# A decode attention kernel: the output matrix wo in four even loads in place of strips over chosen rows

## The chip, the cores and the metric

The kernel runs on one core of one Trainium2 chip. The metric is the device time of one execution in microseconds (us), from the chip's own clock; the median of several runs is given, and the runs of one kernel agree closely. The profile of one execution gives, beside that, its span: the time from its first to its last instruction.

## What is computed

One token passes through an attention block over a cache of 4096 keys and values with 32 heads (A), and through a small MLP with a squared ReLU (B); a sigmoid gate mixes the two.

```
x: 1 x 512; k_cache, v_cache: 32 heads x 4096 x 128; wq: 512 x 4096; wo: 4096 x 512
g = sigmoid(sum(x * gate_w))
q = x @ wq                              # 32 heads of 128
p = softmax(q . k_cache * 128 ** -0.5)  # one row of 4096 for each head
o = p @ v_cache                         # 32 x 128
a = o.reshape(1, 4096) @ wo
h = relu(x @ w1 + b1); b = (h * h) @ w2 + b2       # w1: 512 x 1376
out = g * a + (1 - g) * b
```

All tensors are bf16. The two caches are 33.6 MB each; `wq` and `wo` are 4 MB each, `w1` and `w2` 1.4 MB each.

## The kernel before

The 32 heads are worked in eight quads of four (`NQ`, `R`). A quad's keys are one load of 128 partitions with 32 KB each, and so are its values; the tile `KV` has four slots for them, and `ORDER` gives the order in which SP's queue issues the sixteen loads. A load waits until the load four places earlier has been used up (`done`): for keys until VectorE (DVE) and TensorE (PE) have read them, for values until the product with the probabilities (`pv`) is done.

Half of each quad's scores are made by DVE (`ttr`: multiply and sum of a 128 x 128 block with the query), half by PE: `transposes` into PSUM, a copy by ScalarE (ACT, `evac`), and `scores`. Then follow the maximum (`smax`, `max_rows`, `gmax`, `max_cols`), the exponentials on ACT (`exps`), the denominators (`den`) and `pv` on PE, and `recip` and `norm` on DVE, which leave the four heads' results, times the gate, as four columns of `onorm` (128 x 32, one column a head). Each engine runs its list in order, so where a call stands in the loop over quads and over the eight groups `g` of blocks decides what waits behind it. `PV_BEHIND` says behind which quad each `pv` comes; the last three quads' values are used after the loop.

Before `wo` can be applied, `onorm` has to be laid out as the rows of `wo` lie in SBUF. `wo` has 4096 rows of 1 KB. In this kernel

- rows of heads 0 to 22 (`HX` = 23) go to the tile `W`, whose space the query weights `wq` have left by then. They form 92 strips of 32 KB: a strip is one partition of `W`, with sixteen rows of the lower and sixteen rows of the upper half. Not every partition has a strip. `RUNS` lists 14 loads of strips that GpSimd (POOL) issues, `FIRST` five that SP issues, each with a class `e`, a count, a remainder and a multiple; `place` turns these into partitions. The classes count from 0 to 15 and stand for groups of eight partitions: `32 + 4e + r` and `4e + r` for `e` below 8, `64 + 4e + r` for the outer runs above. POOL issues small loads in between (`dm`, L374), as many rows of 32 bytes as `turns` says, and waits for them at its end;
- rows of head 23 go to `wox`, and those of heads 24 to 31 to `wob_sb` (8 KB on each of 128 partitions), both in a slot of `KV` that the fifth quad's values have left; SP issues them after the last values.

Because the strips' places are irregular, DVE builds at its start a table of which strip lies on which partition (`ramp`, `qv`, `hrow`, `crow`), PE spreads it with three products (L477 to L479), DVE copies it (`sel`), and two comparisons (`mask`, L751) in quad 2 turn it into the selection table `selA`. POOL builds a second, regular one, `selB`, with a memset and an affine select. The result is then brought into place in three parts: `turn_low`, `spread_low` and `out_a(True)` for the lower half in quads 5 and 6; `turn_a`, `spread_a` and `out_a(False)` for the upper half after `pv(5)`; `regroup`, `out_b` and `out_x` after the last `pv`. A turn is a transpose of columns of `onorm` and a copy; a spread is 8 or 16 products with the selection table and a copy; `out_*` are products of 128 x 128 blocks of `wo` with one column, summed in `acc`.

`w1` follows the first values on SP's queue, `w2` comes in five parts (`W2_PARTS`): the first ahead of the last values, the others at the end of the queue. `mlp_out` and `mlp_rows` add the MLP's part to `acc` and `acc4`; a last product turns the sum, DVE copies it to `fin4`, and SP stores it.

The issue order on SP around the change:

```
for n in range(len(ORDER)):
    if n == len(ORDER) - 1:
        load_w2(0)
    load_kv(n)
    ...
    if 4 <= n < 4 + len(FIRST):
        load_first(n - 4)
done("V", NQ - 4)
eng.dma_start(wob_sb, wob_v).then_inc(s_wo, 16)
load_w2(1)
eng.dma_start(wox, A_wo[HX * 128:NA * 128, :]).then_inc(s_wx, 16)
```

Of the kernel before, what the change touches and what calls it, by code (L numbers as in the profile page):

```python
# [5 lines left out]
def bass_gated_mix__gqa_block_cached__dense_activation_squared_relu__decode_kernel(  # L6
# [15 lines left out]
    fp32 = mybir.dt.float32  # L22
# [5 lines left out]
    NH = 32  # L28
# [22 lines left out]
    NA = 24  # L51
    TB = 8

# [6 lines left out]
    W_SLOT = V_SLOT[NQ - 4]  # L60
# [4 lines left out]
    INNER, OUTER, SEAM, WRAP = range(4)  # L65
    RUNS = [(INNER, 4, 12, 0, 2), (INNER, 4, 12, 1, 2),
            (OUTER, 4, 3, 0, 1), (SEAM, 7, 2, 0, 1), (OUTER, 9, 7, 0, 1),
            (SEAM, 7, 2, 1, 1), (WRAP, 15, 2, 1, 1), (OUTER, 1, 2, 1, 1), (OUTER, 3, 2, 1, 1),
            (SEAM, 7, 2, 2, 1), (WRAP, 15, 2, 2, 1), (OUTER, 1, 2, 2, 1),
            (SEAM, 7, 2, 3, 1), (WRAP, 15, 2, 3, 1)]  # L70
    FIRST = [(INNER, 0, 3, 0, 1), (INNER, 0, 3, 1, 1), (INNER, 0, 3, 2, 1), (INNER, 0, 3, 3, 1),
             (OUTER, 0, 2, 0, 1)]
    HX = NA - 1

    NS2 = 4 * HX

    def place(kind, e, k, r, m):
        if kind == INNER:
            return 32 + 4 * e + r, 4 // m, k * m
        if kind == OUTER:  # L80
            return (4 * e if e < 8 else 64 + 4 * e) + r, 4, k
        if kind == SEAM:
            return 28 + r, 68, k
        return r, 124, k

    def turns():
        at, out = 0, []
        for _, e, k, _, _ in RUNS:
            d = (e - at) % 16
            out.append((False, d) if d != 1 else (True, e))  # L90
            at = (e + k) % 16
        return out

    def strips():
        q = 0
        for run in RUNS + FIRST:
            yield (*place(*run), q)
            q += place(*run)[2]

    STRIPS = list(strips())  # L100

# [8 lines left out]
    woa_v = A_wo[0:HX * 128, :].rearrange("(a p t) n -> p a (t n)", a=2, t=16)  # L111
    wob_v = A_wo[NA * 128:NH * 128, :].rearrange("(p t) n -> p t n", t=TB)
# [4 lines left out]
    with ctx:  # L117
# [12 lines left out]
        W2 = W[:, :].rearrange("p (a x) -> p a x", a=2)  # L130
        wo_sb = W[:, :].rearrange("p (t n) -> p t n", t=32)
        wob_sb = KV[:, W_SLOT, 0:TB * DM].rearrange("p (t n) -> p t n", t=TB)
        wox = KV[:, W_SLOT, TB * DM:(TB + 1) * DM]
# [3 lines left out]
        selB = w1_sb[0:NH - NA, 0:2, 0:1024].rearrange("h a (c p) -> h a c p", c=8)  # L137
        selA = w1_sb[0:NA, 2:4, 0:1024].rearrange("h a (c p) -> h a c p", c=8)
# [8 lines left out]
        oA = sb("oA", [NA, 128], bf16)  # L147
        oL = sb("oL", [NA // 2, 128], bf16)
        oB = sb("oB", [NH - NA, 128], bf16)
        o2A = sb("o2A", [128, 32], bf16)  # L150
        o2B = sb("o2B", [128, TB], bf16)
# [3 lines left out]
        dm = xb[:, :, :].rearrange("p t (n a c) -> p (t n) a c", a=2, c=16)  # L155
# [5 lines left out]
        ramp = S[0:1, 0, :]  # L161
        qv = S[0:1, 1, :]
        hrow = S[0:1, 2, 0:NA]
        crow = S[0:1, 2, 32:48]
        sel = sb("sel", [NA, 144], fp32)
# [26 lines left out]
        SEL = pO[0:NA, 256:400]  # L192
# [3 lines left out]
        O2A = pS[0][:, 0:16]  # L196
        OL = pQ[0:NA // 2, 0:64].bitcast(bf16)
        O2L = pQ[:, 64:80]
        O2B = pS[1][:, 0:TB]
# [10 lines left out]
        s_wr = sem("s_wr")  # L210
        s_wx = sem("s_wx")
# [4 lines left out]
        s_wo = sem("s_wo")  # L216
        s_wp = [sem(f"s_wp{n}") for n in range(len(RUNS))]
        s_dm = [sem(f"s_dm{n}") for n in range(len(RUNS))]
# [38 lines left out]
        s_at = sem("s_at")  # L257
        s_ra = sem("s_ra")
        s_qv = sem("s_qv")
        s_sp = sem("s_sp")  # L260
        s_sc = sem("s_sc")
        s_sa = sem("s_sa")
        s_lt = sem("s_lt")
        s_lc = sem("s_lc")
        s_ac = sem("s_ac")
        s_oT = sem("s_oT")
        s_oc = sem("s_oc")
        s_o2 = sem("s_o2")
# [25 lines left out]
        def _(eng):  # L294
# [23 lines left out]
            def load_first(n):  # L318
                if n == 0:
                    eng.wait_ge(s_qps, NQ)  # L320
                p, st, k, q = STRIPS[len(RUNS) + n]
                eng.dma_start(W2[p:p + st * (k - 1) + 1:st, :, :], woa_v[q:q + k, :, :],
                              max_dma_last_dim=16384).then_inc(s_wr, 16)
# [8 lines left out]
# [4 lines that stand above are left out]
                if n == 2:  # L336
                    eng.wait_ge(s_z, 1)
                    eng.wait_ge(s_b2, 1)
                    eng.dma_start(w1_sb[:, :, :], w1_v[:, :, :]).then_inc(s_w1, 16)
                if 4 <= n < 4 + len(FIRST):  # L340
                    load_first(n - 4)
            done("V", NQ - 4)
            eng.dma_start(wob_sb, wob_v).then_inc(s_wo, 16)
            load_w2(1)
            eng.dma_start(wox, A_wo[HX * 128:NA * 128, :]).then_inc(s_wx, 16)
# [8 lines left out]
        def _(eng):  # L354
# [11 lines left out]
            eng.wait_ge(s_qps, NQ)  # L366
            q = 0
            sent = 0
            for n, ((back, d), run) in enumerate(zip(turns(), RUNS)):
                if back:  # L370
                    eng.inc_swdge_sem([], [], mode="reset_dge_cursor")
                if d:
                    src = B_w1[0:d, 0:32].rearrange("p (a c) -> p a c", a=2)
                    eng.dma_start(dm[0:d, sent, :, 0:8], src[:, :, 0:8]).then_inc(s_dm[sent], 16)  # L374
                    sent += 1
                p, st, k = place(*run)
                eng.dma_start(W2[p:p + st * (k - 1) + 1:st, :, :], woa_v[q:q + k, :, :],  # L377
                              max_dma_last_dim=16384).then_inc(s_wp[n], 16)
                q += k
            assert q == STRIPS[len(RUNS)][3] and STRIPS[-1][3] + STRIPS[-1][2] == NS2  # L380
            eng.wait_ge(s_h, 1)
            eng.memset(w1_sb[0:NH - NA, 0:2, 0:1024], 0.0).then_inc(s_sb, 1)
# [4 lines left out]
            for n in range(sent):  # L387
                eng.wait_ge(s_dm[n], 16)
# [6 lines left out]
        def _(eng):  # L395
# [44 lines left out]

            for c in range(QF):
                qb_copy(c)
# [4 lines left out]
            for q in range(NQ):  # L447
                for g in range(GQ):
# [7 lines left out]
                    if g == 5 and q >= 1:  # L456
                        exps(q - 1)
                s_copy(q)
                if q == NQ - 3:
                    eng.wait_ge(s_lt, 1)  # L460
                    eng.activation(oL[:, :], OL, ACT.Copy).then_inc(s_lc, 1)
                    eng.wait_ge(s_lt, 2)
                    eng.activation(o2A[:, 0:16], O2L, ACT.Copy).then_inc(s_lc, 1)
# [4 lines left out]
        def _(eng):  # L468
# [6 lines left out]
            eng.wait_ge(s_qv, len(STRIPS) + 4)  # L475
            eng.wait_ge(s_xf, 1)
            eng.matmul(SEL[:, 0:128], onesf[0:1, 0:NA], qv, start=True, stop=True)  # L477
            eng.matmul(SEL[:, 128:144], hrow, onesf[0:1, 0:16], start=True, stop=False)
            eng.matmul(SEL[:, 128:144], onesf[0:1, 0:NA], crow, start=False, stop=True).then_inc(s_sp, 1)  # L479
# [86 lines left out]
            def turn_low():  # L566
                eng.wait_ge(s_on, 3)
                eng.wait_ge(s_hs, 2)
                eng.transpose(OL, onorm[:, 0:NA // 2], ident[:, :]).then_inc(s_lt, 1)

            def spread_low():
                eng.wait_ge(s_lc, 1)
                eng.wait_ge(s_sb, 2)
                eng.wait_ge(s_sa, 2)
                for c in range(8):
                    mm = eng.matmul(O2L, selA[0:NA // 2, 0, c, :], oL[:, 16 * c:16 * c + 16],
                                    start=(c == 0), stop=(c == 7))
                mm.then_inc(s_lt, 1)

            def turn_a():  # L580
                eng.wait_ge(s_on, NA // R)
                eng.wait_ge(s_ev, GQ * NQ)
                eng.transpose(KP[2][0:NA, 0:128], onorm[:, 0:NA], ident[:, :]).then_inc(s_at, 1)

            def spread_a():
                eng.wait_ge(s_ac, 1)
                eng.wait_ge(s_cp, R * (NQ - 1))
                for c in range(8):
                    mm = eng.matmul(O2A, selA[:, 1, c, :], oA[:, 16 * c:16 * c + 16],
                                    start=(c == 0), stop=(c == 7))  # L590
                mm.then_inc(s_at, 1)

            def out_a(low):
                if low:
                    eng.wait_ge(s_lc, 2)
                    for q in s_wp:
                        eng.wait_ge(q, 16)
                    eng.wait_ge(s_wr, 16 * len(FIRST))
                else:
                    eng.wait_ge(s_ac, 2)  # L600
# [293 lines left out]
```

## Time and profile before

| what | us or share |
|---|---|
| median of 3 runs | 193.64 (193.63 to 193.68) |
| the profiled execution's own time | 193.59 |
| its span | 192.2 |
| DVE busy | 129.0 (67%) |
| PE busy | 124.2 (65%) |
| ACT busy | 99.3 (52%) |
| POOL busy | 19.9 (10%) |
| read from HBM | 78.32 MB, 407 GB/s over the span |

The profile's slices cut the span into forty equal parts; a digit is the busy share in tenths. The row DMA is the mean over the core's sixteen DMA engines, the row under it what they moved. In the windows the columns are the stretch, its length, busy time and count of PE, PE's weight loads, DVE, ACT and POOL, the clock granted to PE, the DMA share and GB/s. The chain of waits goes back from the last instruction, at each step to what released it. Queue q1 holds the loads that SP issues, q0 those of GpSimd, q10 four small ones of ACT; q8 and q14 bring the engines' instructions. Beside these views the trace keeps every DMA packet (start, duration, size, queue) and each step of each load's semaphore, sixteen for a load over 128 partitions.

### The profile page before, as it was taken

What the parts mean: (1) busy time and instruction counts of PE and PEld (TensorE: products, weight loads), DVE (VectorE), ACT (ScalarE), POOL (GpSimd) and SP (SyncE); (2) the same over time, 40 slices, a digit from 0 to 9 for tenths busy, and PEclk for the clock granted to TensorE, in tenths of its full rate; (3) what the DMA queues carried; (4) which work ended last, traced back from release to release, by engine and by line L of the source; (5) the groups of instructions that cost most, each with busy time, mean ns of one, the idle gap of its engine ahead of it and who ended that gap; (6) DMA issues with size and microseconds to landing.
All of it is one profiled execution on the core that took longest, in us unless ns stands there. A gap on an engine that the chain in (4) does not pass through costs nothing.

```text
span 192.2 us, 6534 instructions
## 1 busy us (share of the span) xinstructions
PE 124.2 (65%) x2439; PEld 111.4 (58%) x2441; DVE 129.0 (67%) x1120; ACT 99.3 (52%) x214; POOL 19.9 (10%) x37
## 2 busy tenths in 40 slices
PE   0047378793898826473992849279569667756746
PEld 0023256672888716463991849179569566656635
DVE  1340399999605999999989649999987992100010
ACT  3007289899403897258199119969816963100000
POOL 5000000029946100000000000000000000000000
PEclk9999879788555885555588557957955975555555
DMA  6999999999999999999999999999999999999990
GB/s 218 437 436 436 436 438 426 436 390 446 453 408 440 423 426 423 425 436 413 425 419 426 418 433 430 428 431 433 423 435 433 416 428 426 430 382 418 420 355 28
DMA packets 5118, 78.73 MB, mean 410 GB/s; under 512 B 1349, under 2 KB 1831, under 8 KB 2088
## 3 DMA queue, kind: packets, MB, share of 16 engines
q1 hardware_dynamic: 4050, 75.76, 92.9%
q0 software_dynamic: 1024, 2.56, 3.4%
q8 instruction: 19, 0.31, 0.7%
q14 instruction: 11, 0.09, 0.1%
q10 hardware_dynamic: 14, 0.01, 0.0%
HBM read 78.32 MB, written 0.00 MB: 407 GB/s over the span
## 4 chain that ended last, share of the span: by engine, by line
DMA 48%; DVE 23%; PE 12%; ACT 10%; issue 4%; SPq 1%; DVEq 0%; ACTq 0%
DMA KV<-in_A_k_cache_dram 34%; DVE KV L776 19%; DMA w2a<-in_B_w_dram 14%; ACT kT L419 6%; PE KP L505 6%; PE pO L549 2%; ACT E L437 2%; PE pQ L487 1%; DVE w_sb L751 1%; PE pS L517 1%; DVE S L776 1%; SPq L299 1%; PE pO L646 1%; ACT qb L408 0%; ACT S L425 0%
## 5 line engine op out<-in xcount | busy, mean ns | idle before, releaser
L776 DVE CUSTOM_DVE_ANT_0 KV<-KV,qb 128x128 bf16<-128x128 bf16 x512 | 112.0, 285 | 14.6 <-DMA KV<-in_A_k_cache_dram 14.6
L419 ACT ACTIVATE kT<-KP 128x1024 bf16<-128x1024 bf16 x64 | 62.0, 1025 | 39.5 <-PE KP L505 38.2
L505 PE MATMUL KP<-ident,KV 128*128 128x128 bf16 x512 | 51.0, 268 | 6.4 <-DMA KV<-in_A_k_cache_dram 6.4
L505 PEld LDWEIGHTS KP<-ident,KV 128*128 128x128 bf16 x512 | 42.5, 123 | 8.6 <-DMA KV<-in_A_k_cache_dram 4.1
L517 PE MATMUL pS<-qcol,kT 128*128 128x4 bf16 x512 | 23.5, 167 | 25.3 <-ACT kT L419 24.7
L776 DVE DVE_READ_ACCUMULATOR2_ANT S<- 128x1 f32 x512 | 39.5, 77 | 0.0
L517 PEld LDWEIGHTS pS<-qcol,kT 128*128 128x128 bf16 x512 | 20.7, 103 | 28.0 <-ACT kT L419 27.5
L549 PEld LDWEIGHTS pO<-E,KV 128*128 128x128 bf16 x1024 | 29.4, 105 | 6.6 <-DMA KV<-in_A_v_cache_dram 4.9
L549 PE MATMUL pO<-E,KV 128*128 128x4 bf16 x1024 | 29.1, 166 | 6.1 <-DMA KV<-in_A_v_cache_dram 4.6
L437 ACT ACTIVATE E<-S,nM 32x128 bf16<-32x128 f32 x32 | 18.5, 577 | 0.9
L408 ACT ACTIVATE qb<-pQ 32x128 bf16<-32x128 f32 x20 | 5.4, 268 | 12.6 <-PE pQ L487 12.2
L798 DVE RECIPROCAL rden<-pO 128x4 f32<-128x4 f32 x7 | 1.2, 173 | 14.4 <-PE pO L549 14.4
L374 POOL DMA_DIRECT2D xb<-in_B_w_dram x9 | 5.4, 604 | 38.5 <-PE pQ L487 38.5
L425 ACT ACTIVATE S<-pS 32x64 f32<-32x64 f32 x32 | 6.9, 215 | 4.3 <-PE pS L517 3.7
L437 ACT ACTIVATION_READ_ACCUMULATOR E<-S,nM 32x1 f32 x32 | 8.0, 251 | 0.0
L487 PE MATMUL pQ<-W,xb 128*128 128x512 bf16 x18 | 6.8, 515 | 1.7 <-ACT qcol L413 1.2
L377 POOL DMA_DIRECT2D W<-in_A_wo_dram x14 | 7.9, 565 | 0.0
L477 PE MATMUL pO<-S,onesf 1*24 1x128 f32 x2 | 0.6, 410 | 9.4 <-DVE S L742 9.4
L804 DVE SCALAR_TENSOR_TENSOR onorm<-pO,gcol,rden 128x4 bf16<-128x4 f32 x8 | 1.8, 222 | 6.2 <-PE pO L549 5.9
L525 PE MATMUL pM<-identf,mp 128*1 128x128 f32 x8 | 3.0, 372 | 4.2 <-DVE mp L784 4.2
L477 PEld LDWEIGHTS pO<-S,onesf 1*24 1x24 f32 x2 | 0.1, 119 | 9.5 <-DVE S L742 9.5
L529 PE MATMUL pM<-onesf,dg 1*128 1x1 f32 x16 | 3.4, 281 | 3.0 <-DVE dg L791 3.0
(108 smaller groups left out, 85.3 us busy)
## 6 DMA issues: line engine op xcount, KB each, us to landing
KV<-in_A_k_cache_dram SPq DMA_DIRECT2D x8, 4096.0 KB, 30.3
KV<-in_A_v_cache_dram SPq DMA_DIRECT2D x7, 4096.0 KB, 25.0
W<-in_A_wq_dram SPq DMA_DIRECT2D x1, 4096.0 KB, 12.2
KV<-in_A_v_cache_dram SPq DMA_DIRECT2D x4, 1024.0 KB, 21.1
W<-in_A_wo_dram POOLq DMA_DIRECT2D x2, 768.0 KB, 19.5
w_sb<-in_B_w_dram SPq DMA_DIRECT2D x1, 1376.0 KB, 12.0
w2a<-in_B_w_dram SPq DMA_DIRECT2D x2, 512.0 KB, 28.0
KV<-in_A_wo_dram SPq DMA_DIRECT2D x1, 1024.0 KB, 26.3
```

Source lines behind the costliest of these rows:

```text
L374: eng.dma_start(dm[0:d, sent, :, 0:8], src[:, :, 0:8]).then_inc(s_dm[sent], 16)
L377: eng.dma_start(W2[p:p + st * (k - 1) + 1:st, :, :], woa_v[q:q + k, :, :], max_dma_last_dim=16384).then_inc(s_wp[n], 16)
L408: eng.activation(qb[rows(r), c, :], QR[c][rows(r), r * 128:(r + 1) * 128], ACT.Copy)\
L419: eng.activation(kT[:, n % NT, :], KP[n % 3][:, :], ACT.Copy).then_inc(s_ev, 1)
L425: eng.activation(S[rows(r), q % NS, 0:YQ], S2[rows(r), :, r], ACT.Copy).then_inc(s_cp, 1)
L437: eng.activation(E[rows(r), q % NE, :, r], S[rows(r), q % NS, :], ACT.Exp, bias=nM[rows(r), q:q + 1], scale=SCALE, accum_out=RS[rows(r), h ...
L487: mm = eng.matmul(QR[c], xb[:, t, :], wq_sb[:, t, c * 512:(c + 1) * 512], start=(t == 0), stop=(t == 3))
L505: mm = eng.transpose(KP[n % 3][:, y * 128:(y + 1) * 128], key(q, b), ident[:, :])
L517: mm = eng.matmul(pS[q % 2][:, R * c:R * c + R], kT[:, n % NT, y * 128:(y + 1) * 128], qcol[:, R * q:R * q + R], start=True, stop=True)
L529: eng.matmul(MB[:, q:q + 1], dg[:, q % 2, :], onesf[0:1, 0:1], start=True, stop=True).then_inc(s_mb, 1)
L549: mm = eng.matmul(O[:, R * q:R * q + R], KV[:, V_SLOT[q], b * 128:(b + 1) * 128], E[:, q % NE, COLUMN[b], :], start=(b == 0), stop=(b == N ...
L776: ins = eng.tensor_tensor_reduce(key(q, b), key(q, b), qb[:, q, :], 1.0, 0.0, ALU.mult, ALU.add, S[:, q % NS, c:c + 1])
```

## The change

`wo` is cut into four groups of eight heads (`NG`, `GH`), and each group is one load of 1 MB over 128 partitions with 8 KB runs, all four into `W`. SP issues groups 0, 1 and 2 behind V1, K4 and V2 (`WO_AT`), group 3 behind the last values; head 23's own load is gone. POOL's 14 strip loads and 9 small ones go, and so do DVE's table, PE's three products for it and the comparisons. One selection table, `selB`, serves all groups. Groups 0 and 1 are turned, spread and multiplied in quads 5 and 7 (`GROUP_IN`), with ACT's copies; group 2 after `pv(5)` and group 3 after the last `pv`, with DVE's copies. Turn and spread write into the bank `pM`.

```diff
+    NG = 4
+    GH = NH // NG
+    GROUP_IN = {5: 0, 7: 1}
+    WO_AT = {5: 0, 6: 1, 7: 2}
...
-    woa_v = A_wo[0:HX * 128, :].rearrange("(a p t) n -> p a (t n)", a=2, t=16)
-    wob_v = A_wo[NA * 128:NH * 128, :].rearrange("(p t) n -> p t n", t=TB)
+    wo_v = A_wo.rearrange("(g p t) n -> g p t n", g=NG, t=TB)
...
+        wo_sb = W[:, :].rearrange("p (g t n) -> p g t n", g=NG, t=TB)
...
-            def load_first(n):
-                if n == 0:
-                    eng.wait_ge(s_qps, NQ)
-                p, st, k, q = STRIPS[len(RUNS) + n]
-                eng.dma_start(W2[p:p + st * (k - 1) + 1:st, :, :], woa_v[q:q + k, :, :],
-                              max_dma_last_dim=16384).then_inc(s_wr, 16)
+            def load_wo(g):
+                if g == 0:
+                    eng.wait_ge(s_qps, NQ)
+                eng.dma_start(wo_sb[:, g, :, :], wo_v[g, :, :, :]).then_inc(s_wo[g], 16)
...
-                if 4 <= n < 4 + len(FIRST):
-                    load_first(n - 4)
-            done("V", NQ - 4)
-            eng.dma_start(wob_sb, wob_v).then_inc(s_wo, 16)
+                if n in WO_AT:
+                    load_wo(WO_AT[n])
+            load_wo(NG - 1)
             load_w2(1)
-            eng.dma_start(wox, A_wo[HX * 128:NA * 128, :]).then_inc(s_wx, 16)
...
+            def turn(g, nm):
+                eng.wait_ge(s_on, 2 * g + 2)
+                eng.wait_ge(s_nm, nm)
+                eng.transpose(OT, onorm[:, GH * g:GH * g + GH], ident[:, :]).then_inc(s_ot, 1)
+
+            def spread(g):
+                eng.wait_ge(s_oc, 2 * g + 1)
+                if g == 0:
+                    eng.wait_ge(s_sb, 2)
                 for c in range(16):
+                    mm = eng.matmul(O2, selB[:, c // 8, c % 8, :], oT[:, g, TB * c:TB * c + TB],
                                     start=(c == 0), stop=(c == 15))
+                mm.then_inc(s_ot, 1)
+
+            def out_rows(g):
+                eng.wait_ge(s_oc, 2 * g + 2)
+                eng.wait_ge(s_wo[g], 16)
+                if g == 0:
+                    eng.wait_ge(s_hs, 2)
                 for t in range(TB):
                     for j in range(4):
+                        eng.matmul(acc[:, j:j + 1], wo_sb[:, g, t, j * 128:(j + 1) * 128], o2[:, g, t:t + 1],
+                                   start=(g == 0 and t == 0 and j == 0), stop=False, skip_group_check=True)
...
+                    if g == 6 and q in GROUP_IN:
+                        turn(GROUP_IN[q], q)
+                    if g == 7 and q in GROUP_IN:
+                        spread(GROUP_IN[q])
+                if q in GROUP_IN:
+                    out_rows(GROUP_IN[q])
...
-            turn_a()
-            spread_a()
-            out_a(False)
+            turn(NG - 2, NQ)
+            spread(NG - 2)
+            out_rows(NG - 2)
...
-            regroup()
-            out_b()
+            turn(NG - 1, NQ)
+            spread(NG - 1)
+            out_rows(NG - 1)
             mlp_out(1)
-            out_x()
...
+            def ot_copy(g):
+                eng.wait_ge(s_ot, 2 * g + 1)
+                eng.activation(oT[:, g, :], OT, ACT.Copy).then_inc(s_oc, 1)
...
+            def group(g):
+                eng.wait_ge(s_ot, 2 * g + 1)
+                eng.tensor_copy(oT[:, g, :], OT).then_inc(s_oc, 1)
+                eng.wait_ge(s_ot, 2 * g + 2)
+                eng.tensor_copy(o2[:, g, :], O2).then_inc(s_oc, 1)
```

On ACT, `ot_copy` and `o2_copy` (the same for `O2` into `o2`) stand behind the evacuations of groups 6 and 7 of quads 5 and 7.

## The prediction

> **What bounds the kernel now.** I read the page's slices first, then the windows by stage, the DMA queues, the chain that ended last, and at the end the single packets and landings in the trace.
>
> ```profile
> span 192.2 us, 6534 instructions
> ...
> DMA  6999999999999999999999999999999999999990
> GB/s 218 437 436 436 436 438 426 436 390 446 453 408 440 423 426 423 425 436 413 425 419 426 418 433 430 428 431 433 423 435 433 416 428 426 430 382 418 420 355 28
> ...
> q1 hardware_dynamic: 4050, 75.76, 92.9%
> q0 software_dynamic: 1024, 2.56, 3.4%
> q8 instruction: 19, 0.31, 0.7%
> q14 instruction: 11, 0.09, 0.1%
> ```
>
> ```profile
> 41.50:125.00 83.50, 54.59 (x1045) 51.96 (x1042) 69.91 (x602) 51.13 (x102) 17.21 (x25) 0.65 1.01 427
> 125.00:158.70 33.70, 25.47 (x554) 24.45 (x555) 31.75 (x290) 23.36 (x48) 0.00 (x0) 0.70 1.01 430
> 158.70:184.20 25.50, 16.65 (x506) 15.56 (x504) 2.46 (x12) 2.49 (x9) 0.00 (x0) 0.50 0.99 414
> 184.20:189.50 5.30, 4.06 (x108) 3.50 (x109) 0.76 (x4) 0.00 (x0) 0.00 (x0) 0.50 0.63 226
> ```
>
> The reader is to see that the DMA engines are busy from the first slice to the last but one (last columns of the windows: share 1.01, 1.01, 0.99). No compute engine is: DVE, the busiest, stands at 67%. The chain of waits names DVE and PE often, but behind each sits a K or V load that was waiting in a full queue. Its end is plain:
>
> ```profile
> 160.96 27.32 DMA w2a<-in_B_w_dram
> 188.27 0.05 issue
> 188.32 0.59 PE pQ L637 x16
> ```
>
> So bytes in flight set the end, and the bytes stay: `wo` is 4 MB before and after. What changes is **which DMA engine carries how much**, so I went down to single packets. A 32 KB row takes 1.214 us on one engine (median of 2048), a 16 KB piece 0.612, an 8 KB one 0.313, a 1 KB one 0.046, a semaphore write 0.009. A load of 128 rows puts eight rows on each of sixteen engines; I call these lanes and number them by the classes `e` in `place`. For every load the trace keeps sixteen landing times, one for each lane (us, earliest and latest):
>
> ```
> wq 12.58 12.98 | K1 32.01 33.22 | V0 41.73 44.01 | V3 130.38 133.33
> V6 169.25 172.34 | last part of V7 180.44 184.12 | last of w2 185.61 189.43
> ```
>
> **Why strips are uneven, by the trace.** Counted from `RUNS` and `FIRST`, the 92 strips of 32 KB fall on lanes 0 to 15 as 8, 7, 6, 1, 6, 5, 5, 8, 8, 5, 5, 5, 5, 5, 5, 8. At 2 x 0.612 = 1.224 us a strip, lanes 0 and 3 differ by 8.6 us of work; yet V3, with all strips behind it, lands within 2.95 us. Something else must load lane 3. Without strips a clean lane would have V3 at 12.58 + 11 x 9.715 (K and V loads, eight rows and a semaphore write each) + 3.31 (w1) = 122.75. Lanes with 8 strips then stand at 132.5, those with 5 at 128.9, lane 3 at 124.0. Landed are eight lanes at 130.4 to 131.05, one at 131.47 and seven at 132.55 to 133.33. The extra loads are the instruction refills. Each 16 KB refill of q8 (nineteen; PE has 4880 instructions, 256 go into one) blocks its lane for 1.08 us, and the next 32 KB packet takes 1.70: 1.55 us lost. One such refill on each 5-strip lane gives 130.4, as seen (the 6- and 7-strip lanes fit only roughly). Each 8 KB refill of q14 takes 0.33, and the packet behind it 1.87: 1.0 us lost. Nine of q14's eleven in the span follow DVE's instruction count, some 128 apart (28.2, 41.5, 55.4, 77.1, 92.7, 107.1, 126.4, 139.5, 156.2 us). Seven come before V3: 124.0 + 7 x 1.0 + 0.4 (below) = 131.4, the lane seen at 131.47. From there I follow it by its jumps of 1.0 after 139.5 and 156.2: K7 142.2, V5 162.59, V6 172.34 (the last of sixteen), V7 183.55. So **DVE's refills all fall on lane 3**; q8's go round the others. That step is inferred: the trace does not name a packet's lane.
>
> [...]
>
> **The change, part by part.**
> 1. *Strips out, four even loads in.* Lane 3 loses one strip (1.22), its share of wob (8 x 0.313 + 0.01 = 2.51) and of wox (0.38), together 4.11; it gains 4 x 2.51 = 10.04. That is +5.93 us on the lane already latest at V6. Lanes 0, 7, 8 and 15 lose 12.68 for the same 10.04.
> 2. *GpSimd queue out.* 724 four-byte and some 140 other small packets of q0, 9 ns each: 7.8 us over sixteen lanes, -0.4 us to -0.5 each; lane 3 nets +5.5. POOL's own 23 issues (about 0.6 us each, 41.8 to 55.1) held nobody up: its next work waits for the MLP until 59.2. Gain 0.
> 3. *DVE's table out.* 36 instructions less (33 small ones and a wait before 13 us, two of 1.2 us with a wait at 73). DVE waits for K0 until 22.8 anyway, and later for K5 (8.2 us idle), so 0 on the path. They are 36/128 of a refill on lane 3: -0.28 us on average; whole, it is 0 or -1.0.
> 4. *8 KB runs in place of 16 KB pieces.* Two 8 KB take 0.626 against 0.612, over 16 pairs 0.2 us a lane; already in 1.
> 5. *SP's issues.* Five strip issues (0.67 to 0.88 us) become three of about 0.43 behind V1, K4 and V2; wo(3) follows V7 without its old wait. The 2.5 us that each takes in the queue delays K4 to K7, in place of strips that did the same. Nothing runs dry: on a clean lane V4 ends at 149.7 and V6 with its w2 part at 170.4. V5 waits for DVE on K6 (about 147.7: K6 lands on lane 3 near 126.5, K5's 14.4 us on DVE end near 133, 14.7 more); V7 waits for K7 (landing near 148, done near 164). If that cover went, only clean lanes would idle, and they are 8 us ahead of lane 3: 0.
> 6. *PE and ACT.* turn and spread for groups 0 and 1 go into quads 5 and 7, with a wait for nM; behind them PE queues scores 6 and 7, ACT its S copies, DVE its max. They come some 2 us later (two copies of 0.28, 16 products 0.5, 32 products 1.0). Before, S was complete 1.3 us ahead of DVE, so about 0.7 us of DVE in quad 5, under the cover of 5; taken as 0, bounds 0 and 0.7. The 64 products in quad 6 leave. Group 2 in the tail has 32 products for 64 before, about 0.9 us less, while PE waits for V6: 0.
> 7. *The end.* From V7's last landing (184.12) to the span's end it was 8.08 us; the order stays, only a 0.07 us wait for w2a and four wox products (0.1) go: 7.9.
>
> **Sum.** Lane 3 has V7 complete at 12.58 + 16 x 9.715 + 3.31 + 3 x 2.51 + 1.28 (w2's first part) = 180.1, plus nine refills at 1.0 = 189.1; plus 7.9 = span 197.0; less 0.28. The profiled execution took 193.59 with a span of 192.2, 1.39 around it: **198.1 us**. Against the old lane: 183.55 + 5.5 = 189.05, the same. The runs' median lies 0.05 above the profiled time, which I leave out.
>
> Bounds: eight refills at 0.95 (7.6) to nine at 1.07 (V3's lag of 7.5 over 7; 9.6) and one q8 refill on lane 3 too (11.2) put the time at 197.0 to 200.6; a refill counted by its own packet alone would be 0.33, which lane 3's lag at V3 excludes.
>
> **Rivals.**
> *Lanes alike, not slower.* If refills move round all sixteen lanes, the strips' skew does no work and even loads suit. A clean lane ends at 180.1 + 2.51 + 1.28 + 0.29 + 0.75 = 185.0; refills spread are (19 x 1.55 + 11 x 1.0)/16 = 2.5, one more on the worst 1.55: 189.0 against 189.43, time 193.2. It decides if V3's lane at 131.47 is not lane 3. For it: lanes are unnamed, and K1's lag of 1.2 fits any lane. Against: a skew of 8.6 us that vanishes by V3. [...]
> *Compute turns late as well.* The waits of 6 and K tiles 3 to 5 us later could push DVE past the cover of lane 3 too, at V7: its V6 part ends near 179 and V7 is issued near 164, so it takes 15 us more. Then 200 to 204.
>
> **Chances.** Forecast 0.86, lanes alike 0.09, compute late 0.05. Range 196.2 to 199.9, which holds some nine tenths of the forecast's chance and with it 8 times in 10: its bounds less the top, where q8 would have to hit lane 3 as well, and room below for a cheaper refill. A difference of 0.2% (0.4 us) is about what can be told from no change; the first rival's 193.2 lies at that line, so its 0.09 is split, with a little of the forecast's low end: faster 0.05, same 0.05, slower 0.90.
>
> **What would show it.** Right: the spread of the sixteen landings, 3 to 4 us in the old tail, grows to 8 or 9 with one lane alone behind; V7 complete near 189; DMA share in the last 6 us far below 0.63; no q0 packets; DVE's refills still near nine. Wrong: a spread under 4 us (lanes alike), several lanes late together, or a DMA share clearly below 1 between 125 and 160 us (loads issued late).

## The result, and the profile after

The changed kernel takes 198.39 us (median of four runs, 198.15 to 198.64), the kernel before beside it 193.66: a ratio of 1.0245, 95% interval 1.0232 to 1.0257. The change makes the kernel slower by some 4.7 us. The profiled execution took 198.37 us with a span of 196.9.

The page of the changed kernel, first line, the slices of the DMA engines and their queues:

```profile
span 196.9 us, 6447 instructions
...
DMA  6999999989999999999999999999999999999710
GB/s 233 447 439 453 433 441 423 426 370 449 433 436 431 433 396 459 421 416 439 403 448 443 418 439 426 418 426 431 433 423 421 429 433 431 377 420 422 304 65 6
...
q1 hardware_dynamic: 4296, 78.32, 93.7%
q8 instruction: 19, 0.31, 0.6%
q14 instruction: 11, 0.09, 0.1%
```

Its windows, with the columns as before:

```profile
125.00:158.70 33.70, 23.18 (x446) 22.06 (x442) 30.99 (x283) 24.15 (x51) 0.00 (x0) 0.70 1.00 426
158.70:184.20 25.50, 17.17 (x522) 16.32 (x523) 6.49 (x51) 4.90 (x17) 0.00 (x0) 0.52 1.00 413
184.20:189.50 5.30, 3.31 (x105) 3.14 (x105) 0.18 (x1) 0.00 (x0) 0.00 (x0) 0.50 0.48 181
189.50:194.20 4.70, 3.57 (x103) 3.12 (x101) 0.76 (x4) 0.00 (x0) 0.00 (x0) 0.50 0.07 24
```

The reader is to see three things. GpSimd's queue q0 is gone, and its bytes are in q1 (75.76 + 2.56 = 78.32 MB). Up to 184 us the DMA engines are as full as before (share 1.00), so no load was issued too late. What is new is the end: a share of 0.48 where it was 0.63, and then 4.7 us at 0.07, which is about one engine of sixteen (0.0625). The DMA digits show the same as "710" where they were "990".

The chain of waits of the changed kernel, its last part (start, length, what):

```profile
164.88 24.37 DMA KV<-in_A_v_cache_dram
189.29 0.96 PE pO L467 x30
190.25 0.18 issue
190.44 0.23 PE pO L467 x2
190.75 0.23 DVE onorm L654
...
195.41 0.28 DVE fin L710
```

Before, the chain ended with a part of w2; now it ends with the last part of the last values (V7), and all that follows V7, the normalization, the turn, the spread and the products with `wo`, lies behind it. The sixteen landings of that part and of w2's last, one for each lane, in order of time (us):

```
V7, last part   before  180.44 ... 183.41 183.55 184.12
                after   180.12 ... 183.53 183.55 185.08 189.25
w2, last part   before  185.61 ... 188.74 189.26 189.43
                after   185.02 185.04 185.09 185.18 185.34 185.41 186.55 187.86 ...
                        188.41 189.74 193.84
```

One lane alone is 4.1 us behind the next. Taken in order of time, fourteen of the other fifteen landings of w2's last part come earlier than before and one comes 0.5 us later; only the last lane matters.

### The profile page after: what moved, and what is told of

Same layout as the page of the kernel before. It is cut to its first block, busy times and chain, and to the rows that moved or that the text cites. A ratio compares the mean times of both kernels' runs of the same rounds, so it can differ in the third digit from the quotient of the medians.

```text
span 196.9 us, 6447 instructions
## 1 busy us (share of the span) xinstructions
PE 124.6 (63%) x2432; PEld 111.5 (57%) x2432; DVE 122.4 (62%) x1086; ACT 99.2 (50%) x216; POOL 6.5 (3%) x14
## 3 DMA queue, kind: packets, MB, share of 16 engines
q1 hardware_dynamic: 4296, 78.32, 93.7%
HBM read 78.32 MB, written 0.00 MB: 398 GB/s over the span
## 4 chain that ended last, share of the span: by engine, by line
DMA 37%; DVE 29%; PE 17%; ACT 10%; issue 5%; SPq 1%; DVEq 0%; ACTq 0%
DVE KV L626 25%; DMA KV<-in_A_k_cache_dram 24%; DMA KV<-in_A_v_cache_dram 12%; ACT kT L335 6%; PE KP L423 5%; PE pO L467 4%; PE pQ L405 2%; ACT qb L324 2%; PE pQ L480 2%; ACT E L353 1%; DVE S L626 1%; PE pS L435 1%; SPq L236 1%; PE pQ L476 1%; DVE dg L641 1%
## 5 line engine op out<-in xcount | busy, mean ns | idle before, releaser
L626 DVE CUSTOM_DVE_ANT_0 KV<-KV,qb 128x128 bf16<-128x128 bf16 x512 | 110.2, 283 | 17.9 <-DMA KV<-in_A_k_cache_dram 17.8
L423 PE MATMUL KP<-ident,KV 128*128 128x128 bf16 x512 | 51.7, 270 | 13.4 <-DMA KV<-in_A_k_cache_dram 11.7
L626 DVE DVE_READ_ACCUMULATOR2_ANT S<- 128x1 f32 x512 | 40.0, 78 | 0.0
L405 PE MATMUL pQ<-W,xb 128*128 128x512 bf16 x20 | 7.7, 529 | 12.0 <-DMA W<-in_A_wq_dram 10.8
L405 PEld LDWEIGHTS pQ<-W,xb 128*128 128x128 bf16 x20 | 2.1, 120 | 14.4 <-DMA W<-in_A_wq_dram 10.9
L494 PE MATMUL pM<-oT,w_sb 8*128 8x8 bf16 x64 | 2.3, 163 | 5.4 <-ACT oT L359 4.8
L638 DVE TENSOR_REDUCE gm<-pM 1x4 f32<-1x128 f32 x8 | 2.2, 275 | 5.5 <-PE pM L443 5.5
L447 PE MATMUL pM<-onesf,dg 1*128 1x1 f32 x16 | 3.9, 313 | 2.3 <-DVE dg L641 2.3
L494 PEld LDWEIGHTS pM<-oT,w_sb 8*128 8x128 bf16 x64 | 1.9, 96 | 6.0 <-ACT oT L359 5.0
```

The lines of the kernel that those rows point to most:

```text
L405: mm = eng.matmul(QR[c], xb[:, t, :], wq_sb[:, t, c * 512:(c + 1) * 512], start=(t == 0), stop=(t == 3))
L423: mm = eng.transpose(KP[n % 3][:, y * 128:(y + 1) * 128], key(q, b), ident[:, :])
L447: eng.matmul(MB[:, q:q + 1], dg[:, q % 2, :], onesf[0:1, 0:1], start=True, stop=True).then_inc(s_mb, 1)
L494: mm = eng.matmul(O2, selB[:, c // 8, c % 8, :], oT[:, g, TB * c:TB * c + TB], start=(c == 0), stop=(c == 15))
L626: ins = eng.tensor_tensor_reduce(key(q, b), key(q, b), qb[:, q, :], 1.0, 0.0, ALU.mult, ALU.add, S[:, q % NS, c:c + 1])
```

## The experiments

Twelve kernels were run, all beside the kernel before. The theory was that of the prediction: DVE's instruction refills all go through lane 3, at about 1.0 us of that lane each, and the strips had left that lane free for them. The runs take the refills away or add some, add bytes to chosen lanes, and issue `wo` from another queue; two of them (e11, e12) look at what limits the kernel once the lane's lag is gone.

**Fewer instructions on DVE.** In the changed kernel DVE makes 1 of its 16 blocks a part (e3, below) or 8 (e5); in the kernel before, 1 (e4).

```diff
-                for b in range(PB * j, PB * j + XB):
+                for b in range(PB * j, PB * j + 1):
...
+            eng.memset(S[:, :, YQ:NB], 0.0).then_inc(s_dz, 1)
```

> The changed kernel with 1 of 16 of DVE's blocks in each part of a quad; the other scores of DVE's half are left out (zero). Every load stays. DVE has some 126 instructions in place of 1085, so its eight or nine refills go. Theory: lane 3 loses its lag of 8.8 us, the next lane (last landing 189.7, V7 185.1) sets the end: 185.1 + 7.65 + 1.47 = 194.2. Rival (the even loads or their 8 KB runs cost the time, not the refills): 198.4.

> The same left out in the kernel before. Theory: lane 3 has one strip there and now ends some 8 us before the others, which keep their strips and PE's refills: 193.6, at most 0.5 faster. Rival (DVE's work as such, or its instructions anywhere, sets the pace): as much faster as the changed kernel with the same left out, some 4 us, 189.5.

> The changed kernel with 8 of 16 of DVE's blocks; the other half of DVE's scores is left out (zero). DVE has 574 instructions in place of 1085: four refills fewer. Theory: lane 3's lag shrinks by 4 x 1.0 to about 4.8 us, V7 at 185.2: 194.3, nearly as with one block, since the next lane is 4.2 us behind. Rival (DVE's work or lateness sets it): halfway between one block and all.

Measured: e3 196.05 us (ratio 1.0111, 1.0058 to 1.0163), e5 196.01 (1.0137, 1.0104 to 1.0170), e4 193.54 (0.9993, 0.9982 to 1.0004). The same omission is worth about 2.3 us to the changed kernel and nothing to the kernel before, and leaving out half (e5) is worth as much as leaving out nearly all (e3), which speaks against the rival that DVE's work sets the time (halfway would be 197.2). The landings say why (us; "refills" is the count of q14 in the span):

```
                      refills   V7 complete, next lane   w2's last part, first two ... last two
after                    11     189.25  185.08           185.02 185.04 ... 189.74 193.84
e5, 8 of 16 blocks        7     185.81  184.94           184.83 185.00 ... 189.86 190.39
e3, 1 of 16               3     184.92  183.59           184.95 185.05 ... 189.56 189.58
before                   11     184.12  183.55           185.61 185.66 ... 189.26 189.43
e4, before with 1 of 16   4     184.37  183.88           180.72 185.37 ... 189.10 189.32
```

In e3 the lag of the one lane is gone. In e4 the opposite appears: with four refills in place of eleven, one lane is 4.65 us ahead of all others. The trace doesn't name it, but it fits the lane with one strip: V7 is complete there at 175.57, and the prediction had followed that lane to 183.55 in the kernel before. That is 7.98 us for the eight refills that are missing by then (e4's fourth comes at 188.11). So the uneven strips had filled up about what the refills took. What e3 and e5 miss is the rest of the forecast: with V7 complete 4.33 us earlier, e3 should have come out at 194.2, and its median is 1.8 us more. Its four executions lie between 194.30 and 196.70, those of e5 between 195.42 and 197.06, far wider apart than the changed kernel's; only one execution of each is profiled (195.56 in e3), so what differs between them isn't known. The chain of waits of e3:

```profile
154.30 30.62 DMA KV<-in_A_v_cache_dram
184.92 0.05 issue
184.97 0.96 PE pO L467 x30
185.93 1.80 issue
187.72 0.23 PE pO L467 x2
```

PE stops two products before the end of V7 and waits 1.80 us for nothing that the profile shows, where the changed kernel's chain has 0.18 at the same place. The span agrees: 196.9 - 4.33 + (1.80 - 0.18) = 194.19, and it is 194.2. For e5, with 1.52 us at that place, the same sum gives 194.8, again its span. The trace of e3 has a 16 KB instruction refill of PE that starts at 185.38. This is taken up below.

**The same work in fewer instructions.** e8 leaves nothing out: DVE makes the sixteen products of a part with one instruction and their sums with another.

```diff
-                for b in range(PB * j, PB * j + XB):
-                    c = COLUMN[b]
-                    ins = eng.tensor_tensor_reduce(key(q, b), key(q, b), qb[:, q, :], 1.0, 0.0,
-                                                   ALU.mult, ALU.add, S[:, q % NS, c:c + 1])
+                blocks = KV[:, K_SLOT[q], PB * j * 128:(PB * j + XB) * 128].rearrange("p (b d) -> p b d", d=128)
+                c = COLUMN[PB * j]
+                eng.tensor_tensor(blocks, blocks, qb[:, q, :].unsqueeze(1).to_broadcast([128, XB, 128]),
+                                  ALU.mult).then_inc(s_tt, 1)
+                eng.wait_ge(s_tt, NP * q + j + 1)
+                ins = eng.tensor_reduce(S[:, q % NS, c:c + XB], blocks, AX.X, ALU.add)
```

> The changed kernel, nothing left out: DVE's sixteen multiply-and-sum instructions of a part (two records each) become one product over sixteen blocks and one sum, so some 960 instructions and seven or eight refills go. Theory: lane 3 falls back among the others, 194.2; slower only if DVE's longer pieces make K's slots late. Rival (even loads cost it): 198.4.

Measured: 197.03 us (195.69 to 197.66; ratio 1.0175, 1.0134 to 1.0216). DVE's two groups in e8, busy time and mean ns behind the bar:

```profile
L630 DVE TENSOR_REDUCE S<-KV 128x16 f32<-128x2048 bf16 x32 | 73.1, 2286 | 1.1
L627 DVE TENSOR_TENSOR KV<-KV,qb 128x2048 bf16<-128x2048 bf16 x32 | 38.9, 1215 | 15.1 <-DMA KV<-in_A_k_cache_dram 15.1
```

A part takes 2.29 + 1.22 = 3.50 us, about what its sixteen single instructions took (110.2 / 32 = 3.44), with 64 instructions in place of 512 products and their reads. q14 has 3 refills, and V7 is complete at 185.08, its next lane at 184.13: the lane's lag can be taken away without leaving any work out. Yet of the 4.2 us that V7 gains only 1.4 reach the time, and neither the theory's 194.2 nor the rival's 198.4 was met. The chain of e8 again shows where they stay:

```profile
179.97 2.63 issue
182.60 0.38 PE pM L459 x2
182.98 3.36 PE pO L468 x126
186.34 2.56 issue
188.90 0.23 PE pO L468 x2
```

PE waits twice for some 2.6 us, the second time with all of V7 in place. The refills of PE there start at 180.16 and 186.43, and PE goes on at 182.60 and 188.90: 2.44 and 2.47 us later. The same distance is found at other stops of PE: 182.03 to 184.41 and 187.89 to 190.44 in the changed kernel, 185.38 to 187.72 in e3, 176.24 to 178.59 in the kernel before; nine such places in five kernels lie between 2.34 and 2.60. That PE had run up to the end of its instructions there is a reading of these times; the profile shows only that PE waited for nothing else. In the changed kernel the second of the two stops falls almost wholly into PE's wait for the late lane, so that 0.18 us is left of it. In e8, where PE has no other wait beside it, 2.56 us show.

The next run took work off PE in quad 7 and put it behind the last maximum, to see whether the changed kernel's insertion there holds e8 back:

```diff
-    GROUP_IN = {5: 0, 7: 1}
+    GROUP_IN = {5: 0}
...
             max_cols(NQ - 1)
+            turn(1, NQ)
+            spread(1)
+            out_rows(1)
```

> The batched kernel with group 1's turn, spread and products moved from quad 7 to behind the last maximum, with DVE's copies. Theory (with the refills of DVE gone, PE is late in the tail: in quad 7 it waits 3.5 us for ACT's copies, and it waits for its own refills): 2 to 3 us shorter than the batched kernel, near 194.5, with V7 complete near 185. Rival (the end is set by the loads alone): no change, 197.

Measured: 197.83 us (1.0215, 1.0195 to 1.0235), a miss: V7 is complete at 185.06, as in e8, and w2's last part at 189.70 (e8: 190.42), but what was moved now stands in PE's row at the end, and PE stops for 0.71, 2.90 and 1.19 us on its way. By their chains PE, not the loads, sets the end of e8 and e11; in e3 it is V7's last landing and PE's stop right behind it.

**Does the place of PE's refills decide?** If so, the kernel before should move with them too. Forty idle products at its start, where PE waits for wq, shift them:

```diff
+            for n in range(40):
+                eng.matmul(pM[:, 0:4], ident[:, :], ident[:, 0:4], start=True, stop=True)
```

> The kernel before with 40 additional 128x128 products on PE at the start, while PE waits for wq anyway: all else is the same, every load and every group. What it changes is only where PE's 16 KB instruction refills fall in its stream: 40 instructions earlier in the work. Theory (the tail's end depends on where such a refill falls: an instruction refill costs PE 1.5 to 2.6 us where PE runs without waits, as in the batched kernel): the refill that falls into V7's last part in the kernel before moves, and the tail ends up to 2 us otherwise, about 195.3 us, with the landings of V7 and of w2's last part where they were within 0.5 us. Rival (PE's refills lie beside other work in the tail and only the landings count): 193.6 us, ratio 1.000.

Measured: 193.73 us (1.0005, 0.9995 to 1.0015). The refill of 182.44 starts at 180.66, and what PE waits for changes; first the kernel before, then e12 (total, times, longest, in us):

```profile
PE pO L549 <- DMA KV<-in_A_v_cache_dram: 4.6, 4, 2.1
...
PE pQ L637 <- issue: 2.4, 1, 2.4
...
PE pO L549 <- issue: 1.4, 1, 1.4
```

```profile
PE pO L551 <- issue: 4.1, 4, 1.8
...
PE pO L551 <- DMA KV<-in_A_v_cache_dram: 1.9, 3, 1.1
...
PE pQ L605 <- issue: 1.5, 2, 1.0
```

All of PE's stops for nothing shown (the rows marked issue, these and the shorter ones) add up to 4.9 us in the kernel before and to 6.2 us in e12, 1.3 us more, while the waits for V loads shrink by 2.7 us; V7 is complete at 184.08 (before: 184.12), w2's last part lands at 189.24, and the time stays. The theory put to this run fell, the rival held. But the test is narrow: the moved stop ends at 183.26, still ahead of V7's last landing, so the run shows only that a stop costs nothing when a load behind it ends later. In e3 and e8 PE's last stop ends 2.8 and 3.8 us after V7's last landing, which is why it can cost there. That e8 without its 2.56 us would come near the 194.2 expected is inferred from its chain; a kernel with PE's refills placed otherwise in that tail was not tried.

**More instructions on DVE.** 256 small memsets in DVE's idle time, half at its start, half behind the last maximum, two refills' worth:

```diff
+            for n in range(128):
+                eng.memset(idle[:, n:n + 1], 0.0)
```

> The changed kernel with 256 one-element memsets more on DVE, 128 of them before K0 lands and 128 behind the last maximum, both where DVE waits; bytes and loads as they were. Theory: two refills more on lane 3, 2.0 to 2.1 us longer, 200.4. Rival (refills cost DMA lanes nothing): 198.4.

Measured: 200.10 us (1.0345, 1.0327 to 1.0362). The count of q14 goes from 11 to 13, V7's late lane from 189.25 to 191.13, w2's from 193.84 to 195.76; the lane next to it stays (189.74 to 189.66). That is 0.94 us of one lane for each refill, with no byte of data added, and 0.86 us of the time.

**Bytes on chosen lanes.** If lane 3 is the late one, some bytes on it cost time and the same on others don't. Four loads of 11 KB rows of w1 (0.413 us a row) go into the dead `w1_sb` behind V2, each on the partitions of one class: with four rows each (e9, below) they are meant for lanes 0 to 3, with three rows (e10: `4 * 3 - 3`) for lanes 0 to 2.

```diff
+                    for r in range(4):
+                        a, b = 32 + r, 32 + r + 4 * 4 - 3
+                        eng.dma_start(w1_sb[a:b:4, :, :], w1_v[a:b:4, :, :]).then_inc(s_pad, 16)
```

> Like the run with 68 rows, but each row on a partition of the class its lane fills anyway: four loads behind V2 of four rows of w1 (11 KB each, the same data again), partitions 32 + r + 4e, so four rows on each of lanes 0 to 3. Theory: lane 3 carries 4 x 0.413 = 1.65 us more, 200.0. Rival (bytes alone): 0.18 MB, 0.4 us, 198.8. Rival (any extra load disturbs all lanes, as the 51 rows did): the same time here and with three rows.

> The same with three rows in each of the four loads: lanes 0 to 2 carry 1.65 us more, lane 3 nothing. Theory: no change, 198.4 within 0.3, and with it the extra 2 us of the 51 rows came from their partitions, not from their lanes. Rival: as with four rows.

Measured: e9 199.87 us (1.0322, 1.0302 to 1.0341), e10 198.45 (1.0247, 1.0227 to 1.0267): +1.48 us for 4 x 0.413 = 1.65 us on lane 3, and +0.06 for the same on three other lanes. The landings of the four extra loads show the late lane directly (each load also has one step of its semaphore at its issue, left out here): in e10 twelve come, the last at 103.66 us; in e9 sixteen, twelve of them by 103.45 and the other four, one for each load, from 106.59 to 107.84. V7's late lane lands at 191.22 in e9 and at 189.42 in e10 (189.25 in the changed kernel). The only rows that e9 has beyond e10 are those on the partitions of class 3. So the late lane is that of class 3, and lanes 0 to 2 have time to spare. The counts agree with a lane for each row: sixteen landings for four loads of four rows, twelve for four of three; which engine a row took, the trace doesn't name.

An earlier pair had tried the same with one load of 4 KB rows onto consecutive partitions, 68 rows (e1, below; it landed in four steps) or 51 (e2; three):

```diff
+                    eng.dma_start(w1_sb[:, :, :].rearrange("p t f -> p (t f)")[8:8 + 68, 0:2048],
+                                  wo_v[0, 0:68, 0:4, :].rearrange("p t n -> p (t n)")).then_inc(s_pad, 16)
```

> The changed kernel with one load more behind V2: 68 rows of 4 KB into a dead part of w1_sb, which nothing reads. 68 has 4 as its largest divisor up to 16, so the rows should fall on lanes 0 to 3, 17 each. Theory (lane 3, which takes DVE's refills, is the one that ends last): 17 x 0.159 = 2.7 us longer, 201.1. Rival (all lanes alike, bytes alone count): 0.28 MB at 432 GB/s = 0.6 us, 199.0.

> The same with 51 rows (largest divisor 3): lanes 0 to 2, again 17 rows each. Theory: those lanes have 4 us or more to spare behind lane 3, so no change, 198.4 within 0.3. Rival (bytes alone): 0.21 MB, 0.5 us, 198.9. If lane 3 were not the late one but one of lanes 0 to 2, 201.1.

Measured: e1 204.97 us (1.0588, 1.0572 to 1.0603), e2 200.49 (1.0363, 1.0344 to 1.0381), both slower than either theory had said. While the load ran, from 100 to 105 us, all 32 KB packets were slowed: those that started between 101 and 103 us took 2.1 to 2.4 us, where they take 1.21. Every lane's K5 landed late, the first at 112.53 in e2, at 110.70 in the changed kernel, and lane 3's at 118.93 (e1: 123.31) for 116.55. By the prediction's numbering, rows went here to partitions that their lane doesn't write otherwise; in e9 and e10 they did not, and no lane but the ones loaded was slowed (e10: +0.06 us of the time). The two pairs differ also in the size and number of rows, in their source and in the number of loads, so which of these holds up all lanes wasn't settled. The order of e1 and e2 (4.5 us apart) agrees with a late lane 3, but on account of this side effect the times of the pair alone would show little. The extra load's own landings say more: three in e2, up to 106.59, and four in e1, of which three come up to 106.51 and the fourth only at 113.83. That a load takes as many lanes as the largest divisor up to 16 of its row count is the author's premise in the two expectations. The landings of this case fit it (three for 51 rows, four for 68, three and four for the loads of three and four rows of e10 and e9, sixteen for 96 and for 128 in the kernel before); no run shows it for other row counts.

**Another queue.** Groups 0 to 2 issued by GpSimd instead of SP, as even as before:

```diff
+            for g in range(NG - 1):
+                eng.dma_start(wo_sb[:, g, :, :], wo_v[g, :, :, :]).then_inc(s_wo[g], 16)
```

> The changed kernel with groups 0 to 2 of wo issued by GpSimd at 41 us in place of SP; even loads as they are. Theory: the queue doesn't matter, only what lane 3 carries: 198.4 within 0.3. Rival (it was the second queue, or the earlier start, that made the kernel before fast): towards 193.7.

Measured: 198.51 us (1.0264, 1.0248 to 1.0279), as the changed kernel (198.39). Which queue issues `wo`, and when, is not what costs; how its rows are shared among the lanes is.

No kernel run here that makes the whole computation beats the kernel before. e8 beats the changed kernel by about 1.4 us with all work done. So taking the lane's lag away has won back 1.4 to 2.4 us of the 4.7; what keeps the rest is read from the chains of e3, e5, e8 and e11 (PE's stops) and not shown by a run that removes it.

## Why the prediction was right

*What bounds the kernel, and lane 3.* Right, and no longer inferred: e9 against e10 names the lane, e3 and e5 take its lag away with DVE's instructions, e6 lengthens it, and e4 shows one lane early in the kernel before, by about as much, when most of DVE's refills are gone.

*Step 1, strips out, even loads in (+5.93 on lane 3).* Right: V7 complete was forecast at 189.1 and came at 189.25, 5.70 us after lane 3's 183.55, for a net of 5.5 (that 183.55 is lane 3 is the prediction's own inference, which e4 supports). What other lanes gained is worth nothing. The price of a refill, 1.0 us taken nine times, holds as well: the lag against a clean lane is 189.25 - 180.1 = 9.15 us, 1.02 each; e6 gives 0.94 and e4, by the inference just named, 1.00.

*Step 2, GpSimd's queue.* Right as a zero for the queue: e7 puts `wo` back on it and the time stays. The 0.4 to 0.5 us a lane for the small packets was not tested by itself.

*Step 3, DVE's table (-0.28).* The small term that failed. It was an average over "0 or -1.0", and it was 0: q14 has eleven refills as before. The time is 198.39, where the sum without this term is 198.4; that it meets so closely is partly luck, as V7 came 0.15 us later and the end 0.25 us shorter than forecast.

*Steps 4 and 5, run length and SP's issues.* The DMA share stays at 1.00 up to 184 us, and K7, put at 148, landed at 146.65; V7 was issued at 162.93, put at 164. The cover named there held.

*Step 6, PE and ACT in quads 5 and 7.* The wait came as described (PE stood 2.59 us for ACT's copies) and cost nothing under the late lane.

*Step 7, the end.* 7.9 us after V7 were forecast, 7.65 came (196.9 - 189.25).

*Lanes alike, the first rival.* Out: a spread of 9.13 us with one lane behind. *Compute late as well, the second.* It does not decide here, but something near it waits under the lane: with the lag removed (e3, e5, e8) the time stops at 196 to 197 and not at 194.2. By the chains its cause is another than the rival named: not DVE past its cover, but PE, which near V7's end stops beside its own instruction refill (1.80 us in e3, 1.52 in e5, 2.56 in e8). The prediction counted PE's refills only by what they take from the DMA lanes and not by what they take from PE.

*Two corrections to the working, on which the forecast did not hang.* It put no price on a refill for PE itself; the waits of the kernel before already hold one, PE's 2.4 us at L637 for nothing shown (176.24 to 178.59 above). And it let q8's refills "go round the others". In the changed kernel six lanes end together, at 185.02 to 185.41, and nine from 186.55 on: these six have V7 at 180.12 to 180.56, where a clean lane was put at 180.1, so they show no loss of 1.55 us. PE's refills seem to use nine lanes, and the latest of them ends 4.1 us ahead of lane 3.

## What to carry to other kernels

Where DMA engines are full, look at the sixteen landings of each load and not at the mean share: here one engine 4.1 us behind the rest set the end, and equal loads were not balanced, since that engine also carried instruction refills at about 1.0 us each (0.94 by e6, 1.02 by the lag). An uneven, ugly placement of rows may be the balance; before it is made even, count what else each engine carries, or take instructions away from the engine whose refills sit there. And when such a lag is removed, look next at what stood waiting under it.

## What the runs showed of the hardware that was not expected

- DVE's 8 KB refills load one DMA engine, at 0.94 us of it each: two more of them moved one lane of sixteen by 1.88 us (e6), and with eight fewer than in the changed kernel no lane stands alone (e3). So DVE's instruction count is here a load on one DMA engine.
- PE, where it stops for nothing else, resumes 2.34 to 2.60 us after the start of a 16 KB refill (nine stops in five kernels); while a load ended later still, this was hidden (e12: 1.3 us more of such stops, no change in time).
- A load of 51 rows of 4 KB, 0.21 MB, on consecutive partitions slowed all 32 KB packets from 1.21 us to as much as 2.3 us while it ran and cost 2.1 us (e2 against the changed kernel); four loads of three rows of 11 KB, 0.13 MB, on partitions of the classes that by the prediction's numbering these lanes fill anyway, cost next to nothing (e10, +0.06 us).
